# Attention scores from float32 operands in place of three products of split operands

## The chip, the cores and the metric

The kernel runs on one core of one Trainium2 chip. The metric is the device time in microseconds (us) of that core for one execution, the median of several runs. Engines go by the profile's names: PE (TensorE; PEld is its weight loads), DVE (VectorE), ACT (ScalarE), POOL (GpSimd) and SP (SyncE, which here issues DMAs).

## The reference, cut to what matters

```python
def _attn_ref(q, k, v):                    # (4, 12, 448, 64) each
    S = q.shape[2]
    scale = 1.0 / np.sqrt(q.shape[-1])
    scores = scale * np.matmul(q, k.transpose(0, 1, 3, 2)) - np.log(S)
    attn = 1.0 / (1.0 + np.exp(-scores))
    return np.matmul(attn, v).astype(np.float32)

def reference(**kwargs):
...
    attn_out = _attn_ref(**attn_kwargs)
    B, H, S, D = attn_out.shape
    x = np.ascontiguousarray(attn_out.transpose(0, 2, 1, 3)).reshape(B, S, H * D)
    x = _moe_ref(x=x, **moe_kwargs)
    return _moe2_ref(x=x, **moe2_kwargs)
```

Attention is a sigmoid of scaled scores (no softmax) over 448 positions and 48 heads with a head dimension of 64. The two layers behind it take its output: `_moe_ref` is a gated layer whose first product has 768 x 1024 weights (`w_in`), `_moe2_ref` a layer with cosines and sines of a product, a mix over positions and a last product.

## The kernel before

Heads go in pairs, n = 0 to 23, six pairs to a batch element. Head 0 of a pair lies on partitions 0 to 63 and head 1 on 64 to 127 (`halves`), so the two matmuls of a pair, each over 64 rows, use the two row halves of the array. A pair's keys and queries come in one tile `r` of 128 x 2 x 448 float32 (`load_kq`, L165 to L170, 448 KB, four buffers).

Most products of the kernel are made of split operands. An operand is rounded to the type float32r (`hi`), the rest is put into a second tile (`lo`), and three products hi*hi, hi*lo and lo*hi are summed in PSUM. `split_pair` (L177 to L182) does it on DVE for keys and queries: a copy into `kqh` (L181) and a subtraction into `kql` (through the helper at L56), for 23 of the 24 pairs. Pair 0 (`F32_SCORES`) isn't split: its scores are one float32 matmul per head, straight from `r`. A float32 matmul stands in the trace as two records of each of its weight load and matmul, a float32r one as one.

`scores(t, g)` (L189 to L200) makes the scores of 128 keys (g = 0, 1, 2) by 448 queries for both heads into a PSUM tile of two banks (`pss`), and ACT turns it into a sigmoid, 128 x 896, tile `af` (L186). The last 64 keys of two pairs go together in `end_scores` (L202 to L208), float32 from `r` for all pairs. `begin_attend` (L217) and `attend` (L224) multiply sigmoids and values in float32 into `psa`; ACT copies the result to float32r (L62) and DVE subtracts for the low part (L56). `uv` (lines L65 to L67 and L243 to L245) is the first product of the layer behind, float32r, three products each.

PSUM is four tiles of two banks (`banks`), which `pss`, `pse` (end scores), `psa` and `psd` (uv) take in turn. PE, ACT, DVE and SP follow the order in which the program is written for this stage (`manual_schedule`). It has twelve rounds, r = 0 to 11, of two pairs each. A round: end scores of the next two pairs; loads of the pairs of round r + 3; a piece of weight work; attention of the current two pairs; six score groups (three for each of the next two pairs); then weight work again with the two splits of the pairs of round r + 2 in between; then the uv groups that `UV_BY` allows (none in rounds 0 to 2, two or three in each later one). The weight work ("pieces") takes float64 weights as 64-bit words (`wraw`) and puts float32 together on DVE (L99, L101, L111) and ACT (L106); for `w_in` it also splits it. From some 200 us on, the rest of the layers follows, ordered by a planner except for what the program ties down.

The pool `at` holds all of this stage's tiles of attention; the pools of the next stage take its place in SBUF once it is closed.

Of the kernel before, what the change touches and what calls it, by code (L numbers as in the profile page):

```python
# [10 lines left out]
F32 = mybir.dt.float32  # L11
F32R = mybir.dt.float32r
# [6 lines left out]
B, H, S, D = 4, 12, 448, 64  # L19
# [3 lines left out]
P = 128  # L23
# [10 lines left out]
PIN = 3.1415925  # L34
EPS = 1e-6

F32_SCORES = (0,)
NAF = 6
CH_FROM = 1
NX = 12  # L40
NKQ = 3
LOADS = ((1, 0), (2, 0), (2, 0)) + 8 * ((2, 2),)
UV_BY = (0, 0, 0, 3, 5, 7, 10, 13, 15, 18, 20)
NW = 4
# [6 lines left out]
def net(ctx: ExitStack, tc: tile.TileContext, kq, vd, vl, w_in, w_sp, bsp, w_out, w_th, w_tok, w_ch, out):  # L51
    nc = tc.nc
    ve, se, te = nc.vector, nc.scalar, nc.tensor

    def sub(o, a, b):
        ve.tensor_tensor(out=o, in0=a, in1=b, op=ALU.subtract)  # L56
# [22 lines left out]
    halves = (slice(0, 64), slice(64, P))  # L79
# [71 lines left out]
    at = es_l.enter_context(tc.tile_pool(name="at", bufs=2, reuse_waits="tile"))  # L151
# [3 lines left out]
    def banks(name):  # L155
        return ps_1.tile([P, 2, 512], F32, tag="s", name=name)


    def load_ends(b):

        r = at.tile([P, NP, D], F32, tag="vends", name="vends")
        nc.sync.dma_start(r, vl[b])
        return r

    def load_kq(n):  # L165
        b, p = divmod(n, NP)
        t = {"n": n, "a": {}, "fs": n in F32_SCORES}
        r = t["r"] = at.tile([P, 2, S], F32, tag="kqr", name="kqr", bufs=4)
        nc.sync.dma_start(r, kq[b, p])
        return t  # L170

    def load_v(t):
        b, p = divmod(t["n"], NP)
        t["v"] = at.tile([P, 6, D], F32, tag="vr", name="vr", bufs=4)
        nc.sync.dma_start(t["v"], vd[b, p])

    def split_pair(t):  # L177
        r = t["r"]
        hi = t["h"] = at.tile([P, 2, S], F32R, tag="kqh", name="kqh", bufs=NKQ)
        lo = t["l"] = at.tile([P, 2, S], F32R, tag="kql", name="kql", bufs=NKQ)  # L180
        ve.tensor_copy(hi, r)  # L181
        sub(lo, r, hi)  # L182

    def sigmoid(tag, ps, bufs):
        af = at.tile([P, 2, S], F32, tag=tag, name="af", bufs=bufs)
        se.activation(af, ps[:, :, :S], AF.Sigmoid, bias=bias, scale=1.0 / math.sqrt(D))  # L186
        return af

    def scores(t, g):  # L189

        ps = banks("pss")
        c = slice(g * P, (g + 1) * P)
        if t["fs"]:
            for j, a in enumerate(halves):
                te.matmul(ps[:, j, :S], t["r"][a, 0, c], t["r"][a, 1, :], start=True, stop=True)
        else:
            for n, (w, x) in enumerate(("hh", "hl", "lh")):
                for j, a in enumerate(halves):
                    te.matmul(ps[:, j, :S], t[w][a, 0, c], t[x][a, 1, :], start=n == 0, stop=n == 2)  # L199
        t["a"][g] = sigmoid("af", ps, NAF)  # L200

    def end_scores(ts):  # L202

        ps = banks("pse")
        for i, t in enumerate(ts):
            for j, a in enumerate(halves):
                te.matmul(ps[halves[i], j, :S], t["r"][a, 0, L0:S], t["r"][a, 1, :], start=True, stop=True)
        return sigmoid("afe", ps, 2)  # L208
# [3 lines left out]
    def begin_attend(ts, ends, ae):  # L212

        ps = [banks("psa")[:, 0, :] for _ in ts]
        for i, t in enumerate(ts):
            for j, a in enumerate(halves):
                te.matmul(ps[i][a, :S], ends[halves[i], t["n"] % NP // 2 * 2 + j, :], ae[halves[i], j, :],  # L217
                          start=True, stop=False)
        return ps

    def attend(t, ps):
        for c in range(3):
            for j, a in enumerate(halves):
                te.matmul(ps[a, :S], t["v"][:, 2 * c + j, :], t["a"][c][:, j, :], start=False, stop=c == 2)  # L224
        xf = ps[:, :S]
        X = x_p.tile([P, 2, S], F32R, tag="X", name="X", bufs=NX)
        acopy(X[:, 0, :], xf)
        sub(X[:, 1, :], xf, X[:, 0, :])
        b, p = divmod(t["n"], NP)
        if b % 2 == 0:  # L230
            xl[b // 2, p] = x_p.tile([P, 2, 2, LT], F32R, tag="XL", name="XL", bufs=NP + 2)
        ve.tensor_copy(xl[b // 2, p][:, :, b % 2, :], X[:, :, L0:S].bitcast(F32))
        xs[b, p] = X
# [76 lines left out]
    def load_pieces(n):  # L310
        for _ in range(n):
            if pieces:
                loaded.append(pieces.pop(0))
                loaded[-1].load()

    def begin_pieces(n):

        nonlocal finished
        for w in joined:
            w.part_low()  # L320
        finished += len(joined)
        joined[:] = apart
        apart[:] = loaded
        loaded.clear()
        for w in joined:
            w.join()
        for w in apart:
            w.low()
        load_pieces(n)

    def end_pieces():

        for w in joined:
            w.part_high()
        for w in apart:
            w.high()

    def uv_now(n):
        nonlocal groups
        for _ in range(n):  # L340
            if todo and finished >= (KC if todo[0][1] < 4 else 2 * KC):
                uv(*todo.pop(0))
                groups += 1

    R = B * NP // 2
    groups = 0
    with tc.manual_schedule(engines={mybir.EngineType.PE, mybir.EngineType.Activation, mybir.EngineType.DVE, mybir.EngineType.SP}):
        rounds = {0: [load_kq(i) for i in range(2)]}
        load_pieces(2)
        ends = load_ends(0)  # L350
        rounds[1] = [load_kq(2 + i) for i in range(2)]
        for t in rounds[0] + rounds[1]:
            load_v(t)
        split_pair(rounds[0][1])
        for g in range(3):
            scores(rounds[0][0], g)
        ae = end_scores(rounds[0])
        rounds[2] = [load_kq(4 + i) for i in range(2)]
        for t in rounds[1]:
            split_pair(t)  # L360
        for g in range(3):
            scores(rounds[0][1], g)
        for r in range(R):
            b, q = divmod(r, NP // 2)
            cur, nxt, aft = (rounds.get(r + i) for i in range(3))
            if nxt:
                ends_n = load_ends(b + 1) if q == NP // 2 - 1 else ends
                ae_n = end_scores(nxt)
            if r + 3 < R:
                rounds[r + 3] = [load_kq(2 * (r + 3) + i) for i in range(2)]  # L370
            begin_pieces(1)
            end_pieces()
            ps = begin_attend(cur, ends, ae)
            for i, t in enumerate(cur):
                attend(t, ps[i])
            if aft:
                for t in aft:
                    load_v(t)
            if q == NP // 2 - 1:
                todo += [(b, g) for g in range(8) if g != 3 or b % 2]  # L380
            if not nxt:
                break
            ends, ae = ends_n, ae_n
            for t in nxt:
                for g in range(3):
                    scores(t, g)
            begin_pieces(LOADS[r][0])
            if aft:
                split_pair(aft[0])
            end_pieces()  # L390
            uv_now(min(1, UV_BY[r] - groups))
            if LOADS[r][1]:
                begin_pieces(LOADS[r][1])
            if aft:
                split_pair(aft[1])
            uv_now(min(1, UV_BY[r] - groups))
            if LOADS[r][1]:
                end_pieces()
            uv_now(UV_BY[r] - groups)
        while pieces or loaded or apart or joined:  # L400
            begin_pieces(2)
            end_pieces()
# [83 lines left out]
    for i in range(2):  # L486
        t = pa.tile([P, DH], F32R, name=f"vb{i}", bufs=1)
# [452 lines left out]
```

## Time and profile before

| what | value |
|---|---|
| three runs | 625.8, 627.7, 628.8 us; median 627.7 us |
| profiled execution, its time | 626.07 us |
| profiled execution, its span | 624.3 us |
| PE busy | 612.6 us (98% of the span) |
| DVE busy | 415.8 us (67%) |
| ACT busy | 346.9 us (56%) |
| granted clock of PE | 1.00 |

The profile is of one execution. Busy times overlap. Ends of matmuls are modelled and reach over the start of the next, so an engine that shows as busy can still have been waiting: the starts of instructions tell more than busy shares.

### The profile page before, as it was taken

How to read it: one execution, taken by the hardware profiler on the slowest of the kernel's cores; microseconds unless marked ns; L12 is line 12 of the kernel's file. 1: busy time of each engine (PE TensorE's matmuls, PEld its weight loads, DVE VectorE, ACT ScalarE, POOL GpSimd, SP SyncE). 2: the span in 40 equal slices, each digit the busy share in tenths (PEclk: the TensorE clock that was granted, in tenths of full speed). 3: DMA queues.
4: the chain of work that ended last, by engine and by line, in shares of the span. 5: the costliest groups of instructions: out<-in, count | busy, mean ns of one | idle time of the engine just before them, and what ended most of it. 6: DMA issues, size and time to landing. Idle time of an engine off the chain costs nothing.

```text
span 624.3 us, 9178 instructions
## 1 busy us (share of the span) xinstructions
PE 612.6 (98%) x3296; PEld 507.1 (81%) x3296; DVE 415.8 (67%) x798; ACT 346.9 (56%) x588; POOL 23.8 (4%) x42
## 2 busy tenths in 40 slices
PE   6999999999999999999999999999999999899997
PEld 2455667757776688999999999999999999789996
DVE  3899576627663559794231386797776797688875
ACT  5799466564555425274336486666567566362540
POOL 0000000000000100100000000101101101000000
PEclk9999999999999999999999999999999999999999
DMA  8787588857864685865767612464183123354603
GB/s 308 239 266 233 187 237 277 271 170 250 291 212 144 203 287 180 245 207 181 220 198 230 161 39 65 89 215 114 56 247 92 50 102 126 113 191 134 224 29 134
DMA packets 82675, 112.63 MB, mean 180 GB/s; under 512 B 27842, under 2 KB 69188, under 8 KB 82628
## 3 DMA queue, kind: packets, MB, share of 16 engines
q1 hardware_dynamic: 74820, 99.18, 50.6%
q10 hardware_dynamic: 7808, 12.85, 5.9%
q8 instruction: 26, 0.43, 0.3%
q14 instruction: 21, 0.17, 0.1%
HBM read 68.06 MB, written 32.93 MB: 162 GB/s over the span
## 4 chain that ended last, share of the span: by engine, by line
PE 79%; DVE 11%; DMA 4%; ACT 3%; issue 2%; SPq 0%; POOL 0%; ACTq 0%; POOLq 0%; DVEq 0%
PE psa L224 7%; PE pss L199 6%; PE psd L65 3%; PE psd L243 3%; PE ppo L66 3%; PE ppo L67 3%; PE ppo L65 3%; PE psd L66 3%; PE psd L67 3%; PE psd L245 3%; PE psd L244 3%; PE pt L638 3%; PE pt L639 3%; PE pt L637 3%; PE py L678 3%; PE py L679 3%
## 5 line engine op out<-in xcount | busy, mean ns | idle before, releaser
L186 ACT ACTIVATE af<-pss,bias 128x896 f32<-128x896 f32 x72 | 66.1, 1020 | 2.8 <-PE pss L199 2.8
L637 PE MATMUL pt<-thh,XT 128*128 128x384 f32 x168 | 56.9, 338 | 0.3 <-DVE r L644 0.3
L638 PE MATMUL pt<-thl,XT 128*128 128x384 f32 x168 | 56.9, 338 | 0.0
L224 PE MATMUL psa<-af,vr 128*64 128x448 f32 x288 | 56.8, 543 | 0.0
L639 PE MATMUL pt<-thh,XT 128*128 128x384 f32 x168 | 56.8, 338 | 0.0
L224 PEld LDWEIGHTS psa<-af,vr 128*64 128x64 f32 x288 | 19.6, 137 | 36.3 <-issue 35.2
L62 ACT ACTIVATE ev<-psd 128x448 f32<-128x448 f32 (+1 forms) x30 | 17.0, 568 | 52.5 <-PE psd L67 26.0
L111 DVE SCALAR_TENSOR_TENSOR wq<-wraw,wq 128x384 int32<-128x384 int32 (+2 forms) x51 | 28.7, 594 | 23.7 <-ACT wraw L106 23.6
L65 PE MATMUL psd<-X,wih 128*128 128x448 f32 x96 | 35.6, 371 | 0.0
L106 ACT ACTIVATE wraw<-wraw 128x384 f32<-128x384 f32 (+2 forms) x51 | 29.6, 604 | 10.7 <-DVE wq L99 7.4
L66 PE MATMUL ppo<-g,wbh 128*128 128x448 f32 x96 | 35.2, 366 | 0.0
L67 PE MATMUL ppo<-g,wbl 128*128 128x448 f32 x96 | 35.1, 366 | 0.0
L65 PE MATMUL ppo<-g,wbh 128*128 128x448 f32 x96 | 35.1, 366 | 0.0
L67 PE MATMUL psd<-X,wil 128*128 128x448 f32 x96 | 35.1, 365 | 0.0
L66 PE MATMUL psd<-X,wih 128*128 128x448 f32 x96 | 35.1, 365 | 0.0
L56 DVE TENSOR_TENSOR X<-psa,X 128x448 fp32r<-128x448 f32 x24 | 15.0, 624 | 27.8 <-ACT X L62 27.8
L648 ACT ACTIVATE m<-r 128x384 f32<-128x384 f32 x28 | 14.6, 520 | 32.5 <-DVE r L646 32.5
L637 PEld LDWEIGHTS pt<-thh,XT 128*128 128x128 f32 x168 | 31.5, 188 | 1.1 <-DVE r L644 0.7
L638 PEld LDWEIGHTS pt<-thl,XT 128*128 128x128 f32 x168 | 31.6, 188 | 0.4
L101 DVE SCALAR_TENSOR_TENSOR wq<-wraw,wq 128x384 int32<-128x384 int32 (+2 forms) x51 | 30.6, 600 | 1.8
L639 PEld LDWEIGHTS pt<-thh,XT 128*128 128x128 f32 x168 | 31.5, 188 | 0.0
L62 ACT ACTIVATE xr<-xp 128x768 uint16<-128x768 uint16 x28 | 28.4, 1066 | 0.5 <-ACT x L62 0.5
(287 smaller groups left out, 1583.9 us busy)
## 6 DMA issues: line engine op xcount, KB each, us to landing
kqr<-in_kq SPq DMA_DIRECT2D x24, 448.0 KB, 4.6
wraw<-in_w_in SPq DMA_DIRECT2D x12, 512.0 KB, 5.3
x_d<-x ACTq DMA_DIRECT2D x24, 224.0 KB, 3.3
xb<-x_d SPq DMA_DIRECT2D x4, 1344.0 KB, 7.7
xp<-xa SPq DMA_DIRECT2D x56, 96.0 KB, 2.5
y_d<-y SPq DMA_DIRECT2D x24, 224.0 KB, 2.1
out_t<-o SPq DMA_DIRECT2D x24, 224.0 KB, 2.0
vr<-in_vd SPq DMA_DIRECT2D x24, 192.0 KB, 4.5
```

Source lines behind the costliest of these rows:

```text
L62: se.activation(o, a, f)
L65: te.matmul(ps, wh, xh, start=first, stop=False)
L66: te.matmul(ps, wh, xl, start=False, stop=False)
L67: te.matmul(ps, wl, xh, start=False, stop=last)
L101: ve.scalar_tensor_tensor(out=self.q, in0=self.hi, scalar=-(2 ** 31), in1=self.q, op0=ALU.bitwise_and, op1=ALU.bitwise_or)
L106: se.activation(self.lo.bitcast(F32), self.hi.bitcast(F32), AF.Copy, scale=2.0 ** -112)
L186: se.activation(af, ps[:, :, :S], AF.Sigmoid, bias=bias, scale=1.0 / math.sqrt(D))
L199: te.matmul(ps[:, j, :S], t[w][a, 0, c], t[x][a, 1, :], start=n == 0, stop=n == 2)
L224: te.matmul(ps[a, :S], t["v"][:, 2 * c + j, :], t["a"][c][:, j, :], start=False, stop=c == 2)
L637: te.matmul(o, t[:, k, 0, :], thh[:, k, hs], start=k == 0, stop=False)
L638: te.matmul(o, t[:, k, 0, :], thl[:, k, hs], start=False, stop=False)
L639: te.matmul(o, t[:, k, 1, :], thh[:, k, hs], start=False, stop=k == KC - 1)
```

## The change

`scores` makes one float32 product per head for every pair, as it did for pair 0, from `r` as it was loaded. `split_pair`, its tiles `kqh` and `kql` (three buffers each) and its four calls go, and `r` gets eight buffers in place of four.

```diff
-F32_SCORES = (0,)
 NAF = 6
...
-NKQ = 3
...
     def load_kq(n):
         b, p = divmod(n, NP)
-        t = {"n": n, "a": {}, "fs": n in F32_SCORES}
-        r = t["r"] = at.tile([P, 2, S], F32, tag="kqr", name="kqr", bufs=4)
+        t = {"n": n, "a": {}}
+        r = t["r"] = at.tile([P, 2, S], F32, tag="kqr", name="kqr", bufs=8)
         nc.sync.dma_start(r, kq[b, p])
         return t
...
-    def split_pair(t):
-        r = t["r"]
-        hi = t["h"] = at.tile([P, 2, S], F32R, tag="kqh", name="kqh", bufs=NKQ)
-        lo = t["l"] = at.tile([P, 2, S], F32R, tag="kql", name="kql", bufs=NKQ)
-        ve.tensor_copy(hi, r)
-        sub(lo, r, hi)
...
         c = slice(g * P, (g + 1) * P)
-        if t["fs"]:
-            for j, a in enumerate(halves):
-                te.matmul(ps[:, j, :S], t["r"][a, 0, c], t["r"][a, 1, :], start=True, stop=True)
-        else:
-            for n, (w, x) in enumerate(("hh", "hl", "lh")):
-                for j, a in enumerate(halves):
-                    te.matmul(ps[:, j, :S], t[w][a, 0, c], t[x][a, 1, :], start=n == 0, stop=n == 2)
+        for j, a in enumerate(halves):
+            te.matmul(ps[:, j, :S], t["r"][a, 0, c], t["r"][a, 1, :], start=True, stop=True)
         t["a"][g] = sigmoid("af", ps, NAF)
...
-        split_pair(rounds[0][1])
...
-        for t in rounds[1]:
-            split_pair(t)
...
-            if aft:
-                split_pair(aft[0])
...
-            if aft:
-                split_pair(aft[1])
```

## Rows read from the trace of the kernel before

**Rows 1.** Page, part 1: busy us (share of the span) xinstructions.

```profile
PE 612.6 (98%) x3296; PEld 507.1 (81%) x3296; DVE 415.8 (67%) x798; ACT 346.9 (56%) x588; POOL 23.8 (4%) x42
```

**Rows 2.** Stretches: busy us of PE, PEld, DVE, ACT, POOL; granted clock, DMA share, GB/s.

```profile
4.00:20.00 16.00, 14.41 (x80) 6.09 (x82) 7.98 (x12) 10.56 (x13) 0.00 (x0) 1.00 0.96 339
20.00:54.00 34.00, 34.00 (x234) 16.97 (x236) 31.28 (x53) 30.96 (x43) 0.00 (x0) 1.00 0.76 242
54.00:200.00 146.00, 145.72 (x874) 99.42 (x872) 89.55 (x172) 84.72 (x124) 0.00 (x0) 1.00 0.71 228
```

**Rows 3.** PE's waits, 0 to 215 us: total, times, longest.

```profile
PE pss L195 <- DMA kqr<-in_kq: 3.9, 1, 3.9
PE pse L207 <- DMA kqr<-in_kq: 1.5, 1, 1.5
```

**Rows 4.** PE's waits from 200 us to the end: the longest of four.

```profile
PE pa__5430 L832 <- DVE y L59: 1.3, 1, 1.3
```

**Rows 5.** PE by time, round 4: start, duration, instruction.

```profile
70.38 0.98 PE L207 MATMUL pse<-kqr 64*64 64x448 f32 x8
71.18 0.93 PE L217 MATMUL psa<-af,vends 64*64 64x448 f32 x8
72.04 4.73 PE L224 MATMUL psa<-af,vr 128*64 128x448 f32 x24
76.70 0.47 PE L199 MATMUL pss<-kqh 64*128 64x448 f32 x2
77.42 0.37 PE L199 MATMUL pss<-kqh 64*128 64x448 f32 x2
78.03 0.37 PE L199 MATMUL pss<-kqh 64*128 64x448 f32 x2
...
79.89 0.37 PE L199 MATMUL pss<-kqh 64*128 64x448 f32 x2
80.61 0.47 PE L65 MATMUL psd<-X,wih 128*128 128x448 f32 x1
```

**Rows 6.** Float32 instructions of single lines: ns min/median/max, first and last start.

```profile
L195 PEld LDWEIGHTS pss<-kqr x12: 218/329/335, 3.9 to 7.1; 64*128 64x128 f32 x12
L195 PE MATMUL pss<-kqr x12: 536/946/1110, 3.9 to 7.5; 64*128 64x448 f32 x12
L207 PE MATMUL pse<-kqr x96: 536/546/587, 8.0 to 192.0; 64*64 64x448 f32 x96
```

**Rows 7.** PE by time, round 1.

```profile
31.03 0.47 PE L199 MATMUL pss<-kqh 64*128 64x448 f32 x2
...
34.87 0.98 PE L207 MATMUL pse<-kqr 64*64 64x448 f32 x8
35.76 1.87 PE L217 MATMUL psa<-af,vends 64*64 64x448 f32 x8
37.56 4.73 PE L224 MATMUL psa<-af,vr 128*64 128x448 f32 x24
```

**Rows 8.** ACT by time, the sigmoids of round 1.

```profile
32.01 5.50 ACT L186 ACTIVATE af<-pss,bias 128x896 f32<-128x896 f32 x6 [0.31 <-PE pss L199]
```

**Rows 9.** PE by time, round 3.

```profile
53.41 0.48 PE L199 MATMUL pss<-kqh 64*128 64x448 f32 x2
...
55.12 0.47 PE L199 MATMUL pss<-kqh 64*128 64x448 f32 x2 [0.20 <-DVE X L56]
...
57.92 0.50 PE L243 MATMUL psd<-wih,X 128*128 128x512 f32 x1
```

**Rows 10.** DVE's groups of the split: busy us, mean ns, idle before.

```profile
L56 DVE TENSOR_TENSOR kql<-kqr,kqh 128x896 fp32r<-128x896 f32 x23 | 25.1, 1092 | 0.8
L181 DVE CAST kqh<-kqr 128x896 fp32r<-128x896 f32 x23 | 14.3, 621 | 10.6 <-DMA kqr<-in_kq 10.6
```

**Rows 11.** SP by time: DMA issues at the start.

```profile
4.25 4.66 SPq L175 DMA_DIRECT2D vr<-in_vd  x4
10.79 0.81 SPq L169 DMA_DIRECT2D kqr<-in_kq  x2
```

## The prediction

> **What bounds the kernel now.** I began with the page's busy shares: PE is busy for 98% of the span, DVE for 67%, ACT for 56% [rows 1]. That is an average, so I cut the time into stretches [rows 2]. The change touches only the attention stage, to about 202 us. Before 20 us the DMA engines are full (a share of 0.96, 339 GB/s) and PE has gaps. From 20 to 54 us (rounds 0 to 2, no uv work) DVE and ACT are busy for 31 of 34 us, beside a PE that shows no gap. From 54 to 200 us PE is the only full engine: DVE has work for 90 of 146 us and ACT for 85.
>
> Then PE's own waits. Up to 215 us two matter, both for the first loads [rows 3]; after 200 us the longest of four is 1.3 us [rows 4]. So PE's order sets the end, and what a matmul is made longer by reaches the end unless PE was secretly waiting where it is put. Modelled ends hide such waits, so I read starts, round by round.
>
> Round 4 stands for rounds 4 to 10, seven of them [rows 5]. Six score groups run from 76.70 to 80.61 us, 3.91 us: 0.61 to 0.63 us a group, with 0.1 us more at the first and at the last, where the array's layout changes. Uv work follows at once, and nothing there waits for ACT or DVE beyond that 0.1 us.
>
> Round 1 stands for rounds 0 to 2 and differs [rows 7, 8]. From the first score to the first L224 takes 6.53 us against 5.57 us in round 4 (3.91, then 0.80 and 0.86 for L207 and L217). ACT explains it: six sigmoids take 5.50 us from 32.01 us, some 0.9 us apart, the four PSUM tiles fill, and the second half of L217 waits for the fifth sigmoid. There the score block has about 0.9 us of cover.
>
> Round 3 lies between: its block takes 4.51 us (53.41 to 57.92 us) because group three waits for a DVE subtraction [rows 9].
>
> **What the change removes.** On DVE 23 casts and 23 subtractions, 14.3 + 25.1 = 39.4 us [rows 10], about 3.4 us a round. PE is full over the same time and waits for DVE only in round 3, so I cost this at nothing but there. What hides it is PE's own work; without that cover it would be worth the most in rounds 0 to 2. Even there little is to be had: PE's own work for such a round, if it waited for nothing, would with the new block (below) be 4.72 + 0.80 + 0.86 + 4.66 = 11.04 us, against a period of 11.19 us now (from 31.03 us to the end of L224's block, 37.56 + 4.66 us [rows 7, 5]).
>
> On PE 414 float32r matmuls go (23 pairs, three groups, two heads, three products).
>
> **What it adds.** 138 float32 matmuls in their place, 276 records, two of each pair of heads side by side. How long is a group of these? The exact form occurs only in the first 8 us, for pair 0 [rows 6]: 12 records start from 3.93 to 7.5 us and the next line follows at about 8.0 us, six steps of two records in 4.0 us. Their durations are 946 ns in the median and 536 ns at the least; the later float32 matmuls of L207, on the same number of columns, take 536 to 587 ns. Though the granted clock shows 1.00 there, the start so ran at about half of the later rate, as at 1.2 GHz of the two levels. The two heads do overlap: 12 x 842 ns of records would be 10.1 us one after the other.
>
> For the later rate I take the nearest float32 rows of round 4 [rows 5]. L224 has 24 records, two side by side, so 12 steps from 72.04 to 76.70 us, 4.66 us with the layout change at either end: 0.388 us a step. L207 has 8 records, four side by side, two steps in 0.80 us; L217 two in 0.86 us. A score block is 12 steps: 4.66 us by L224, 4.80 by L207, 5.16 by L217. The low bound is L224 less the two layout changes of 0.1 us, 4.46 us. L224 is the nearest, with the same number of steps and a layout change at both ends; I add 0.06 us, as the middle groups now vary from 0.61 to 0.63 us, which I put down to the step into a new PSUM tile. So 4.72 us for 3.91 us: **+0.81 us a block**, between +0.55 and +1.25. Weight loads (218 ns at the later rate [rows 6]) fit in a step of 0.388 us, so I add nothing for them.
>
> **The sum.**
> - Rounds 4 to 10: 7 x 0.81 = +5.7 us (3.9 to 8.8).
> - Round 3: 4.72 for 4.51 us, as the DVE subtraction that it waits for comes earlier, with 3.4 us less ahead of it in DVE's queue: +0.2 us (-0.1 to +0.65).
> - Rounds 0 to 2: the first sigmoid starts some 0.1 us later (a first group of about 0.8 us for 0.72), and the chain of sigmoids covers the rest: 3 x 0.1 = +0.3 us. If the cover fails, 3 x 0.81 = +2.4; at best, 0.
> - Pair 1, before round 0: three groups, about +0.4 us, covered by the 1.5 us for which PE then waits for `kqr` [rows 3]: 0, or +0.4.
> - Eight buffers: the loads of pairs 4 to 7 need not wait for a buffer. Pairs 4 and 5 are issued at 10.79 us though SP was done with `vr` at 8.91 [rows 11]. They go out earlier, behind the same loads as now, so I expect nothing: PE is not waiting for a load after the first 14 us. If they take bandwidth from `kqr` of pairs 2 and 3 or from `vr`, which are under way, one such load at 339 GB/s is 448 KB / 339 = 1.3 us later: 0 to +1.3. Later SP isn't held up by a load of keys, so the weights behind it come sooner; no PE wait hangs on them: 0.
> - Scores wait for a DMA in place of DVE: by then the load is two rounds old, so 0. ACT's work is the same.
> - `at` shrinks by two tiles of 3.5 KB a partition, so the next stage's tiles lie over others. Its first loads over the old place follow the last attention in the program's order, and both move alike: 0. The planner may order the later stages a little otherwise: 1 us either way.
>
> Sum: 5.7 + 0.2 + 0.3 = **+6.2 us**. After 202 us PE goes on without a gap [rows 4], so all of it arrives at the end. Against the profiled execution that is 626.1 + 6.2 = 632.3 us; this execution was 1.6 us under the median of 627.7 us, from which the sum is 633.9. I take **633.0 us**, between them.
>
> **The rivals.** About 0.5% (3.1 us) is what a measurement of this kernel can tell from no change.
>
> *All covered (no change).* If ACT's chain held PE in the later rounds as in rounds 0 to 2, every block would cost 0.1 us: 11 x 0.1 = +1.1 us, 628. For it: sigmoids 0.9 us apart are slower than groups of 0.78 us. Against it: in round 4 uv starts 0.1 us behind the last score and needs one PSUM tile where round 1 needs three; ACT catches up during the two or three uv groups.
>
> *Float32 is cheaper than three products (faster).* It decides at 0.61 us a group: if a group cost one step of 0.388 us, a block would be about 2.5 us, 1.4 us less, and seven rounds give 9.8 us; with round 3's 2.0 us, the block of rounds 0 to 2 being held by ACT, 626.1 - 11.8, about 614 us. For it: a third of the products are left. Against it: each record has its own step, and L224 shows 12 steps for 12 float32 products of 448 columns in pairs. The Trainium skill has both readings: "Perfetto Trace Analysis", section "Engine Utilization", halves the array's output rate for FP32_LOW_HIGH, which taken for the whole product is this rival at an estimate of 614 us, while "FP8 and Floating Point Precision", section "TensorE Precision Notes", counts four passes for true FP32. The trace bears out the four: two records of about 0.388 us a pair against 0.204 us for one float32r step (0.61 us a group, three steps).
>
> *Dearer still (slower).* Steps as in L217 (0.43 us), cover failing in rounds 0 to 2 and a start disturbed by early loads: 8.8 + 0.65 + 2.4 + 1.3 = +13 us, 639. Against it: L217 ends in a layout change after only two steps, which twelve steps spread.
>
> **How the numbers follow.** Forecast (+3.3 to +10 us) 0.67; dearer still 0.13; all covered 0.14; faster 0.06. So slower by over 0.5%: 0.80; within: 0.14; faster: 0.06. The range runs from a sum at the low bounds with half of the covered case, 628.5, to 638.5, short of the dear case at its full price.
>
> **What would show it.** After the change: no L181, DVE about 376 us busy; score blocks in rounds 4 to 10 of 4.7 us with steps of 0.375 to 0.39 us; rounds 0 to 2 with a period near 11.3 us; no wait for DVE in round 3; whatever PE does after 202 us some 6 us later. The prediction is wrong if a group takes under 0.65 us, if uv in rounds 4 to 10 turns out to start behind a sigmoid, or if PE finds new waits for `kqr` in the first 20 us.

## The result and the profile after

The changed kernel takes 632.8 us in the median of four runs (632.5 to 634.1), the kernel before 627.4: a ratio of 1.0091, with a 95% interval of 1.0062 to 1.0120. It is slower. The prediction was 633.0 us, in a range of 628.5 to 638.5. A second pair (`changed_again` below), beside 29 runs of the kernel before, gave a ratio of 1.0082 (1.0059 to 1.0105).

The profiled execution took 632.99 us, its span 631.0. Here are its busy shares (part 1 of the page) and its stretches, against [rows 1, 2]:

```profile
PE 619.6 (98%) x3158; PEld 495.5 (79%) x3158; DVE 377.9 (60%) x752; ACT 346.6 (55%) x588; POOL 24.0 (4%) x42
```

```profile
4.00:20.00 16.00, 14.84 (x72) 5.57 (x72) 3.10 (x6) 10.35 (x12) 0.00 (x0) 1.00 0.96 349
20.00:54.00 34.00, 34.00 (x194) 13.69 (x192) 21.77 (x41) 30.77 (x43) 0.00 (x0) 1.00 0.73 250
54.00:200.00 146.00, 146.00 (x758) 89.80 (x758) 64.17 (x139) 82.60 (x121) 0.00 (x0) 1.00 0.69 225
```

DVE lost 38 us, some 30% of its work to 200 us, and the kernel got longer. PE, full before, is full after, with 138 records fewer and 7 us more. Round 4 on PE, in order of time, against [rows 5]:

```profile
71.39 0.98 PE L193 MATMUL pse<-kqr 64*64 64x448 f32 x8
72.19 0.93 PE L203 MATMUL psa<-af,vends 64*64 64x448 f32 x8
73.05 4.73 PE L210 MATMUL psa<-af,vr 128*64 128x448 f32 x24
77.71 4.78 PE L185 MATMUL pss<-kqr 64*128 64x448 f32 x24
82.42 0.47 PE L63 MATMUL psd<-X,wih 128*128 128x448 f32 x1
```

The score block runs from 77.71 to 82.42 us: 4.71 us for 3.91. Its 24 records last as long as the 24 of L210 above them within 0.05 us, and uv starts right behind, as before. Round 1 on PE, and ACT's sigmoids in it, against [rows 7, 8]:

```profile
31.49 4.78 PE L185 MATMUL pss<-kqr 64*128 64x448 f32 x24
36.20 0.98 PE L193 MATMUL pse<-kqr 64*64 64x448 f32 x8
37.00 1.24 PE L203 MATMUL psa<-af,vends 64*64 64x448 f32 x8
38.17 0.60 PE L210 MATMUL psa<-af,vr 128*64 128x448 f32 x2
```

```profile
32.62 5.50 ACT L177 ACTIVATE af<-pss,bias 128x896 f32<-128x896 f32 x6 [0.47 <-PE pss L185]
```

Here the block is as much longer (4.71 us for 3.84), but L203 now takes 1.17 us for 1.80: it waited for a sigmoid before, and most of the block's 0.87 us has gone into that wait. From the first score to the first L210 it is 6.68 us for 6.53. Six sigmoids still take 5.50 us; the first starts 1.13 us behind the first score for 0.98, and that 0.15 us is what the round gets longer by.

In round 3 the block runs from 54.17 to 58.88 us, 4.71 for 4.51, and the wait for DVE of [rows 9] is gone. PE's waits, to 215 us and after 200 us, against [rows 3, 4]:

```profile
PE pss L185 <- DMA kqr<-in_kq: 4.0, 1, 4.0
PE pse L193 <- ACT af L177: 1.1, 1, 1.1
```

```profile
PE pa__5062 L811 <- DVE y L57: 1.4, 1, 1.4
```

The wait of 1.5 us for keys in pair 1 is now one of 1.1 us that ends with a sigmoid (in the second profile of the changed kernel, 0.9 us for keys again). No other wait is new. SP's issues at the start, against [rows 11]:

```profile
4.27 4.76 SPq L173 DMA_DIRECT2D vr<-in_vd  x4
10.91 3.23 SPq L167 DMA_DIRECT2D kqr<-in_kq  x4
14.34 0.33 SPq L88 DMA_DIRECT2D wraw<-in_w_in  x1
```

The loads of pairs 4 and 5 are not issued sooner, 10.91 us for 10.79, though they have free buffers now. In both kernels SP's wait ahead of them (1.8 us before, 1.9 after) ends when a load of weights (`wraw`) lands.

### The profile page after: what moved, and what is told of

The parts are those of the page before. It is cut to its first block, busy times and chain, and to the rows that moved or that the text cites. A ratio compares the mean times of both kernels' runs of the same rounds, so it can differ in the third digit from the quotient of the medians.

```text
span 631.0 us, 8829 instructions
## 1 busy us (share of the span) xinstructions
PE 619.6 (98%) x3158; PEld 495.5 (79%) x3158; DVE 377.9 (60%) x752; ACT 346.6 (55%) x588; POOL 24.0 (4%) x42
## 4 chain that ended last, share of the span: by engine, by line
PE 83%; DVE 7%; DMA 5%; ACT 3%; issue 1%; SPq 0%; POOL 0%; ACTq 0%; POOLq 0%; DVEq 0%
PE psa L210 9%; PE pss L185 8%; PE psd L63 3%; PE psd L229 3%; PE ppo L63 3%; PE ppo L64 3%; PE ppo L65 3%; PE psd L64 3%; PE psd L65 3%; PE psd L230 3%; PE psd L231 3%; PE pt L617 3%; PE pt L618 3%; PE pt L616 3%; PE py L657 3%; PE py L658 3%
## 5 line engine op out<-in xcount | busy, mean ns | idle before, releaser
L185 PE MATMUL pss<-kqr 64*128 64x448 f32 x288 | 59.6, 560 | 4.0 <-DMA kqr<-in_kq 4.0
L210 PE MATMUL psa<-af,vr 128*64 128x448 f32 x288 | 56.8, 543 | 0.0
L185 PEld LDWEIGHTS pss<-kqr 64*128 64x128 f32 x288 | 27.4, 192 | 35.2 <-issue 28.5
L210 PEld LDWEIGHTS psa<-af,vr 128*64 128x64 f32 x288 | 19.6, 137 | 36.3 <-issue 36.1
L616 PEld LDWEIGHTS pt<-thh,XT 128*128 128x128 f32 x168 | 31.5, 188 | 1.2 <-DVE r L623 0.8
```

What stands on the lines that cost most here:

```text
L616: te.matmul(o, t[:, k, 0, :], thh[:, k, hs], start=k == 0, stop=False)
```

## Where the time went

Starts on PE add up the whole difference. The first score of round 0 starts at 20.15 us for 19.84, the last attention (its first matmul, L203, L217 before) at 215.50 for 209.26. The recorded expectations call this last point the end of attention.

| piece | after less before, us |
|---|---|
| start, to the first score of round 0 | +0.31 |
| rounds 0 to 2 (34.02 for 33.57) | +0.45 |
| block of round 3 | +0.20 |
| blocks of rounds 4, 5, 6, 8, 9, 10 (4.71 for 3.85 to 3.91) | +4.88 |
| block of round 7 (4.88 for 4.68) | +0.20 |
| uv of all rounds | +0.20 |
| attention stage with the start | +6.24 |
| later stages | +0.5 |
| span (631.0 for 624.3) | +6.7 |

For the experiments two lengths are taken from each profile: the **attention stage**, from the first score of round 0 to the start of the last attention, and the **later part**, from the uv block behind that attention to the end of the span. The start is in neither. The ratio is to the kernel before on the same chip, with its 95% interval.

| run | attention stage, us | later part, us | ratio |
|---|---|---|---|
| before | 189.42 | 409.5 | |
| before_again | 189.51 | 413.5 | 1.0011 (0.9992 to 1.0031) |
| after | 195.35 | 410.0 | 1.0091 (1.0062 to 1.0120) |
| changed_again | 195.32 | 411.2 | 1.0082 (1.0059 to 1.0105) |
| splits_kept | 195.56 | 412.0 | 1.0130 (1.0108 to 1.0153) |
| four_buffers | 219.51 | 411.6 | 1.0492 (1.0461 to 1.0523) |
| fourth_product | 198.49 | 411.1 | 1.0159 (1.0134 to 1.0184) |
| float32_early | 189.68 | 414.6 | 1.0072 (1.0049 to 1.0096) |
| float32_early_again | 189.78 | 411.1 | 1.0024 (1.0004 to 1.0044) |
| float32_late | 194.88 | 410.2 | 1.0064 (1.0041 to 1.0087) |
| one_product | 194.43 | 411.4 | 1.0036 (1.0004 to 1.0068) |
| late_copy | 189.25 | 409.3 | 0.9977 (0.9948 to 1.0007) |
| after_late_copy | 195.15 | 409.7 | 1.0057 (1.0024 to 1.0090) |
| early_and_late_copy | 188.80 | 415.8 | 1.0016 (0.9999 to 1.0033) |

The attention stage repeats within 0.1 us for each of the three programs that were profiled twice. The later part does not: 409.5 and 413.5 us for the very same kernel. What an edit of the attention stage does is therefore read from that stage, and the ratio only says whether it can be seen in the whole.

## The experiments

**Is DVE's relief worth anything?** The changed kernel, with the splits left in and nothing reading them.

```diff
+    def split_pair(t):
+        r = t["r"]
+        hi = at.tile([P, 2, S], F32R, tag="kqh", name="kqh", bufs=1)
+        lo = at.tile([P, 2, S], F32R, tag="kql", name="kql", bufs=1)
+        ve.tensor_copy(hi, r)
+        sub(lo, r, hi)
...
+        split_pair(rounds[0][1])
...
+        for t in rounds[1]:
+            split_pair(t)
...
+            if aft:
+                split_pair(aft[0])
...
+            if aft:
+                split_pair(aft[1])
```

> Float32 scores as in the change, but DVE still splits all 23 pairs into high and low tiles that nothing reads. Theory A (the change's cost is the longer score blocks where PE is the bound; the 39 us taken from DVE bring nothing but the wait in round 3): between 0 and 0.8 us above the changed kernel, 633.0 to 633.8 us; score blocks of rounds 4 to 10 stay at 4.71 us, only round 3's block is over 4.71. Theory B (freeing DVE won time, and the blocks cost more than the net shows): at least 2 us above the changed kernel, 635 us or more.

The two groups of DVE work are back (by line):

```profile
L54 DVE TENSOR_TENSOR kql<-kqr,kqh 128x896 fp32r<-128x896 f32 x23 | 25.1, 1092 | 0.8
...
L179 DVE CAST kqh<-kqr 128x896 fp32r<-128x896 f32 x23 | 14.3, 622 | 10.4 <-DMA kqr<-in_kq 10.3
```

The block of round 4 runs from 77.22 to 81.93 us, 4.71 us as in the changed kernel. 39.4 us of DVE work cost the stage 0.21 us (195.56 for 195.35), all of it in round 3, whose block took 4.93 us for 4.71. The ratio is 0.4% above the changed kernel's: its interval overlaps that of the first pair and just misses that of the second (1.0105 against 1.0108), on a chip whose runs of the kernel before were faster (625.5 us). In time it is 1.0 us above the changed kernel, between theory A's 0.8 and theory B's 2. The profile puts 2.0 us more into the later part, where PE, DVE and ACT follow the order of the kernel before; whether the splits have a share in that is not shown. For the attention stage theory A stands and theory B falls.

**Do passes count, or the type?** The kernel before with a fourth product.

```diff
-            for n, (w, x) in enumerate(("hh", "hl", "lh")):
+            for n, (w, x) in enumerate(("hh", "hl", "lh", "ll")):
                 for j, a in enumerate(halves):
-                    te.matmul(ps[:, j, :S], t[w][a, 0, c], t[x][a, 1, :], start=n == 0, stop=n == 2)
+                    te.matmul(ps[:, j, :S], t[w][a, 0, c], t[x][a, 1, :], start=n == 0, stop=n == 3)
```

> The kernel before with a fourth product, low by low, for the 23 split pairs: the number of passes that theory A ascribes to one float32 product, without float32. Theory A (passes count, not the type): a group is 4 x 0.204 = 0.82 us, a block 5.1 us for 3.9; six full blocks +7.1 us, rounds 7 and 3 +0.5 each, rounds 0 to 2 some +0.3 each: +9 us, 636.4 us. If float32 itself were what is dear, a further step in each group would cost less than the change: under 632 us.

Round 4 on PE, the first record of groups one, two and three, and uv:

```profile
78.04 0.47 PE L199 MATMUL pss<-kqh 64*128 64x448 f32 x2
...
78.97 0.37 PE L199 MATMUL pss<-kqh 64*128 64x448 f32 x2
...
79.79 0.37 PE L199 MATMUL pss<-kqh 64*128 64x448 f32 x2
...
83.19 0.47 PE L65 MATMUL psd<-X,wih 128*128 128x448 f32 x1
```

A group takes 0.82 us and a block 5.15; the stage grew by 9.07 us, as forecast. One float32 product of a pair of heads, 0.75 us a group without the layout changes (two steps of 0.376 us in the trace after), lies between three float32r products (0.61) and four (0.82).

**Where does it cost, where is it covered?** Float32 for pairs 0 to 7 alone, and for pair 0 and 8 to 23 alone. Both have six buffers for `r`, and split only what is not float32.

```diff
-F32_SCORES = (0,)
+F32_SCORES = tuple(range(8))
...
-        r = t["r"] = at.tile([P, 2, S], F32, tag="kqr", name="kqr", bufs=4)
+        r = t["r"] = at.tile([P, 2, S], F32, tag="kqr", name="kqr", bufs=6)
...
-            if aft:
+            if aft and not aft[0]["fs"]:
                 split_pair(aft[0])
```

```diff
-F32_SCORES = (0,)
+F32_SCORES = (0,) + tuple(range(8, 24))
```

> The kernel before with float32 scores for pairs 0 to 7 alone (pair 1 and rounds 0 to 2, where ACT's chain of sigmoids covers PE), six buffers for keys and queries; the other pairs split. Theory A: rounds 0 to 2 have periods of 11.34 us for 11.19 (+0.45 us), the start +0.3 at most, and round 3's wait for DVE goes (-0.6): 627.4 us within 0.5 us, no change. If the cover doesn't hold, 20 groups at 0.17 us make +3.4 us: 630.8 us.

> The counterpart of the run with early pairs: the kernel before with float32 scores for pair 0 and pairs 8 to 23 (rounds 3 to 10), six buffers; pairs 1 to 7 split. Theory A: blocks of 4.71 us in rounds 4 to 10, so six times +0.80 and +0.2 in round 7, round 3 +0.2 to +0.8: +5.5 us when attention ends, near the whole change. If the change's cost lay in the first rounds or in the loads of the start, under +2 us. The later stages have moved by up to 5 us between the runs so far with nothing changed in them, so the attention stage is read from its own starts.

Round 1 of the early run and round 4 of the late run, on PE:

```profile
30.23 4.78 PE L195 MATMUL pss<-kqr 64*128 64x448 f32 x24
...
36.91 4.73 PE L224 MATMUL psa<-af,vr 128*64 128x448 f32 x24
```

```profile
76.83 4.78 PE L195 MATMUL pss<-kqr 64*128 64x448 f32 x24
81.55 0.47 PE L65 MATMUL psd<-X,wih 128*128 128x448 f32 x1
```

Early: from the first score to the first L224 it is 6.68 us, as in the changed kernel. The stage grew by 0.26 us: a period of 11.34 us in round 0, as theory A had it, and 0.13 us back in round 3, where theory A had 0.6. Late: +5.46 us. The two together make 5.72 of the change's 5.93 us. The cost is in the rounds with uv work, and the cover in the others holds.

The early run's time missed its expectation all the same: 0.7% up where no change was expected, 630.5 us where 630.8 stood for a cover that doesn't hold. The stage shows that the cover held. The profile ends the last attention 0.7 us sooner than before, and takes 5.1 us more in the later part. So it was run once more, and the kernel before too.

> The run with float32 for pairs 0 to 7 alone once more. In the first run the attention stage ended 0.7 us sooner than before, yet the time was 0.7% up, since the later stages took 414.6 us for 409.5. If that is a property of this program (its other layout in SBUF and other times of loads), again 413 us or more and a ratio of 1.006 or more; if it was the day of that chip, 409 to 412 us and a ratio within 0.5% of 1.

> The kernel before once more, for a second profile: how much its later stages differ between executions with nothing changed. First profile: 409.5 us from the last block of uv to the end. If they vary by themselves, between 409 and 412 us; if they are steady and the differences of other runs come from their edits, 409.5 within 0.2 us. Ratio 1.000.

> The changed kernel once more, beside its own runs of the kernel before, for a second profile and a narrower interval. Theory A: attention ends (second half of the last L203) near 215.2 us, 6 us later than before; the later stages, whose instructions are the same in the same order, within 1.5 us of the kernel before; +6 to +7 us in all, a ratio of 1.010. If the later stages had been changed by the edit, their part would come out 0.5 us longer again.

The start of the last attention and of the uv block behind it on PE, in the second profile of the kernel before:

```profile
209.23 0.98 PE L217 MATMUL psa<-af,vends 64*64 64x448 f32 x8
...
214.80 0.47 PE L65 MATMUL psd<-X,wih 128*128 128x448 f32 x1
```

It reaches the last attention at 209.23 us, as in its first profile (209.26), and its span is 4.0 us longer: 413.5 us from 214.80 us on, for 409.5. In the second run of the early variant the later part fell from 414.6 to 411.1 us and the ratio to 1.0024. So the later part varies by some 4 us without an edit, and the 5.1 us can't be read as the edit's. The largest of PE's waits after 216 us, in the second profile of the kernel before, stands at another line than in [rows 4]:

```profile
PE pt L637 <- DVE r L644: 2.1, 2, 1.9
```

Behind such a wait the granted clock can fall. These are the stretches behind the wait of 1.9 us at L637, in the second profile of the kernel before, and behind one of 2.3 us at L834, in the first of the early variant (in the second, behind one of 1.8 us, it stays at 1.00):

```profile
512.00:516.00 4.00, 4.00 (x16) 3.93 (x16) 4.00 (x10) 3.48 (x7) 0.00 (x0) 0.63 0.24 86
552.00:556.00 4.00, 4.00 (x13) 3.55 (x13) 2.56 (x5) 0.00 (x0) 0.00 (x0) 0.57 0.78 251
```

In the first of them 18 matmuls of L637 to L639 take 4.81 us for 3.27 in the first profile, so 1.5 of the 4.0 us come with the lower clock and the rest with waits. The early variants meet this more often than the kernel before. All three of their profiles have a wait of 1.8 to 2.3 us at L834 (L839 with the late copy), where the first profile of the kernel before has 0.4 us. A mean granted clock under 0.998 stands in 12 of the 16 runs of the early variant, in 6 of 12 of the early variant with the late copy (below), and in 15 of the 70 runs of the kernel before in these experiments. In the second early run those eight took 630.2 us in the mean and the four others 627.9, as in the kernel before on that chip (a median of 628.0). Whether early float32 causes this, and what makes those chains late in one execution and not in another, was not tested.

**Do the eight buffers matter?** The changed kernel with four.

```diff
-        r = t["r"] = at.tile([P, 2, S], F32, tag="kqr", name="kqr", bufs=8)
+        r = t["r"] = at.tile([P, 2, S], F32, tag="kqr", name="kqr", bufs=4)
```

> The changed kernel with four buffers for keys and queries in place of eight. Theory A: no PE wait hangs on these loads after the start, so 632.8 us within 1 us, though the loads of round r + 3 now wait for the scores of round r. Theory C (the early loads that eight buffers allow disturb the start): attention begins again at 15.2 us in place of 15.5, and the time is 0.3 us lower. A third way, that the weights queued on SP behind the waiting loads come late and hold ACT and then PE in rounds 0 to 3: 2 to 10 us above the changed kernel.

The stage grew by 24.2 us over the changed kernel. The order of the program puts the loads for round r + 3 ahead of the scores of round r. With four buffers those scores must have read the tile before the load can start. SP's issues show it held up from 10.39 us:

```profile
10.39 14.23 SPq L167 DMA_DIRECT2D kqr<-in_kq  x4
24.68 1.50 SPq L88 DMA_DIRECT2D wraw<-in_w_in  x1
```

The weights behind these loads are issued at 24.68 us in place of 14.34. Waits of 20 to 80 us:

```profile
DVE wq L97 <- DMA wraw<-in_w_in: 32.0, 6, 8.3
...
PE pss L185 <- DVE X L54: 9.7, 3, 4.0
```

DVE waits for the weights, its subtraction that frees a PSUM tile stands behind them, and PE waits for that tile: the third way of the expectation, at more than twice its upper price. In rounds 1 to 3 the score blocks take 9.9 to 10.8 us, and the granted clock falls with PE's waits:

```profile
30.00:34.00 4.00, 2.86 (x14) 0.71 (x10) 3.41 (x7) 2.06 (x3) 0.00 (x0) 1.00 0.42 169
34.00:38.00 4.00, 2.15 (x8) 1.01 (x10) 3.31 (x7) 3.88 (x7) 0.00 (x0) 0.78 0.00 0
```

**Why did round 7 cost so little?** Its block took 4.68 us before the change. In DVE's order of time there (kernel before) a copy waits 6.6 us for uv, with the subtraction behind it that frees a PSUM tile. The block doesn't wait for that subtraction itself, which starts 1.2 us after the block's end (139.54 us). Its last three groups start 0.9 us apart, near the pace of the sigmoids, as if one tile too few were free. First PE's fourth and fifth group, then DVE:

```profile
136.85 0.47 PE L199 MATMUL pss<-kqh 64*128 64x448 f32 x2
...
137.75 0.47 PE L199 MATMUL pss<-kqh 64*128 64x448 f32 x2
```

```profile
140.55 0.23 DVE L232 CAST XL<-X 128x128 fp32r<-128x128 f32 x1 [6.62 <-PE psd L245]
140.69 0.62 DVE L56 TENSOR_TENSOR X<-psa,X 128x448 fp32r<-128x448 f32 x1
```

The copy was moved behind both subtractions, in the kernel before and in the changed one.

```diff
-        ve.tensor_copy(xl[b // 2, p][:, :, b % 2, :], X[:, :, L0:S].bitcast(F32))
         xs[b, p] = X
+
+    def ends_x(t):
+        b, p = divmod(t["n"], NP)
+        ve.tensor_copy(xl[b // 2, p][:, :, b % 2, :], xs[b, p][:, :, L0:S].bitcast(F32))
...
                 attend(t, ps[i])
+            for t in cur:
+                ends_x(t)
```

> The kernel before with the copy of the last positions (L232) of both pairs moved behind both subtractions (L56) of a round. In round 7 this copy waits 6.6 us for uv, and the second subtraction, which frees a PSUM tile, stands behind it. Theory A: this is why round 7's block takes 4.68 us before the change and hid most of its cost; the block falls to 3.91 us and attention ends 0.8 us sooner. If the tile isn't what the block waits for, 4.68 us as before.

> The changed kernel with the same move of the copy. Theory A: round 7's block of 4.88 us falls to 4.71 us only, as float32 groups now set it, 0.2 us. If the tile still decides, a larger fall. The rest of the attention stage is as in the changed kernel: it ends 6.0 us later than in the kernel before.

DVE and PE in round 7 of the kernel before with the copy moved, then PE in the changed one:

```profile
135.91 0.62 DVE L56 TENSOR_TENSOR X<-psa,X 128x448 fp32r<-128x448 f32 x1 [1.63 <-ACT X L62]
```

```profile
135.22 0.47 PE L199 MATMUL pss<-kqh 64*128 64x448 f32 x2
...
139.13 0.50 PE L246 MATMUL psd<-wih,XL 128*128 128x512 f32 x1
```

```profile
137.94 4.78 PE L185 MATMUL pss<-kqr 64*128 64x448 f32 x24
142.65 0.50 PE L232 MATMUL psd<-wih,XL 128*128 128x512 f32 x1
```

The subtraction comes at 135.91 us, the block takes 3.91 us (135.22 to 139.13) and 4.71 us with float32: it was the tile. The stage gained only 0.17 us in the kernel before, not 0.8, as round 3's block took 5.11 us for 4.51 in this run. PE waits 1.00 us there for DVE's subtraction (0.20 us in [rows 9]); DVE had waited 0.65 us for weights ahead of it, at 46.00 us, which it didn't in the profile of before. Whether the moved copy has a part in that was not tested. In the changed kernel it gained 0.20 us, as expected.

**Does less work on PE reach the end?** One product in place of three.

```diff
-            for n, (w, x) in enumerate(("hh", "hl", "lh")):
+            for n, (w, x) in enumerate(("hh",)):
                 for j, a in enumerate(halves):
-                    te.matmul(ps[:, j, :S], t[w][a, 0, c], t[x][a, 1, :], start=n == 0, stop=n == 2)
+                    te.matmul(ps[:, j, :S], t[w][a, 0, c], t[x][a, 1, :], start=n == 0, stop=n == 0)
```

> The kernel before with the first of the three products alone (high by high) for the 23 split pairs; it leaves out the two others, so the scores have the precision of the rounded operands. It asks how far shorter PE blocks reach the end. Theory A: PE's part of a block falls from 3.9 to 6 x 0.204 + 0.2 = 1.4 us, but uv then waits for the third sigmoid, some 3.3 us behind the block's start, so a block gains only 0.6 us: 7 x 0.6 = 4.2, and rounds 0 to 3 some 1.5 more: about -5 us against the kernel before. If PE alone decided, -2.5 us in each of 11 blocks: -27 us.

Both forecasts fell: the stage got 5.0 us longer, with two thirds of the score work of 23 pairs gone. The blocks did what theory A said (3.41 us in round 4, set by the third sigmoid): rounds 0 to 2 and the blocks behind them gained 4.1 us. The loss lies behind the blocks, where uv took 9.1 us more. Round 3 on PE in order of time, then the stretches of 51 to 68 us and, last, the block of round 4:

```profile
53.63 0.47 PE L199 MATMUL pss<-kqh 64*128 64x448 f32 x2 [1.77 <-DVE X L56]
54.30 0.69 PE L199 MATMUL pss<-kqh 64*128 64x448 f32 x4 [0.20 <-ACT af L186]
...
56.10 0.80 PE L243 MATMUL psd<-wih,X 128*128 128x512 f32 x1 [0.15 <-ACT af L186]
56.69 0.63 PE L244 MATMUL psd<-wil,X 128*128 128x512 f32 x1
57.12 0.63 PE L245 MATMUL psd<-wih,X 128*128 128x512 f32 x1
```

```profile
51.00:56.00 5.00, 2.76 (x14) 1.08 (x12) 4.38 (x10) 4.75 (x8) 0.00 (x0) 0.88 0.89 330
56.00:60.00 4.00, 3.90 (x9) 3.13 (x10) 3.80 (x7) 4.00 (x7) 0.00 (x0) 0.50 0.66 214
60.00:64.00 4.00, 4.00 (x15) 3.19 (x15) 3.90 (x8) 0.96 (x2) 0.00 (x0) 0.80 0.38 98
64.00:68.00 4.00, 4.00 (x19) 3.30 (x18) 0.78 (x1) 0.60 (x1) 0.00 (x0) 1.00 0.17 66
...
77.00:81.00 4.00, 2.65 (x17) 1.16 (x14) 2.77 (x7) 3.41 (x5) 0.00 (x0) 1.00 0.52 182
```

PE waited between its groups (busy 2.76 of 5 us), the granted clock fell to 0.50, the lower of its two levels (1.2 of 2.4 GHz), and uv behind it ran at 0.43 us a matmul, for 0.23 in the kernel before, until some 61.4 us: 15.05 us of uv for 12.45. The same follows in rounds 6, 7, 9 and 10 (14.10, 13.20, 14.09 and 9.06 us for 12.48, 11.62, 12.48 and 7.49). The kernel before shows 1.00 in all these stretches. But the blocks of rounds 4, 5 and 8 wait as well (PE busy 2.65 of 4 us in round 4), and there the clock stays at 1.00 and uv takes 7.49, 7.50 and 7.63 us for 7.49. So a thinned block was followed by the lower clock in five rounds of eight; what tells them apart was not tested. The Trainium skill ("TensorE: Matmul & The Clock Gate", section "What's actually happening") has an activity monitor set the clock by how busy the engine has been, with the throttled state as the default. This run agrees in the five rounds, the lower clock behind the thinned block and 1.00 once uv had run on; the three others don't show it.

**What the runs point to.** Float32 in rounds 0 to 2 (with round 3's lighter DVE queue) and the late copy, the rest split: the diffs of the early run and of the late copy in one kernel.

> What the runs point to as the quickest attention stage: float32 for pairs 0 to 7 where ACT covers it (no splits there, and no wait for DVE in round 3) and the copy L232 moved behind both subtractions (round 7's block at 3.91 us); the rest split as before. Theory A: attention ends 1.4 us sooner than in the kernel before, at 207.8 us; the whole 0.2% faster if the later stages stay as they are, which is below what the median can tell.

The last attention starts at 207.76 us, 1.5 us sooner than in the kernel before, where 1.4 were expected; but 0.9 us of that is an earlier start (18.96 us for 19.84), which varies without an edit (18.89 and 19.75 us in the two profiles of the early variant). The stage is the shortest of all, 188.80 us. The time is not: 1.0016, from 0.9999 to 1.0033, with 415.8 us in the later part of its profile, whose clock shows 0.57 at 552 to 556 us as above. It beats the changed kernel and not the one before.

## Why the prediction was right

Point by point, by its own steps:

- *What bounds the kernel*: PE's order. Right: work taken from DVE brought 0.2 us to the stage, and work put on PE came out at its end wherever PE was the full engine.
- *The price of a group*, taken from L224 at 4.72 us a block: 4.71 us. L224's row gave it though it has other weights and another layout of the array. The 0.06 us that was added for new PSUM tiles was right by luck: the steps between tiles are 0.376 us like the others, and what the block has over L210's is its first step (77.71 to 78.19, 0.48 us for 0.43). The Trainium skill counts four passes for true FP32 ("FP8 and Floating Point Precision", section "TensorE Precision Notes"); the group of 0.75 us is 3.7 float32r steps of 0.204 us, near that.
- *Seven blocks of +0.81*: +5.08 us, not 5.7. The step that was off is "Round 4 stands for rounds 4 to 10": round 7 took 4.68 us already, for a reason that the trace of before showed in DVE's order of time.
- *Rounds 0 to 2*, +0.3: +0.45, and covered by ACT's chain as said; the run with early pairs alone shows the same. *Round 3*, +0.2: +0.20.
- *Pair 1 and the start*, 0: +0.31 us in one profile and, in the second pair, the first score of round 0 at 19.68 us for 19.72. The +0.31 arises by 8.27 us (7.96 before), in pair 0, which the change leaves as it was. Pair 1 cost nothing, as said: from its first score to the next end scores it is 3.60 us for 3.61.
- *Eight buffers, nothing*: right that they brought nothing. The reason given, that four loads would go out earlier, was wrong for pairs 4 and 5: they go out as late with free buffers, since SP waits for a load of weights to land ahead of them, not for a buffer. What the prediction did not say is that the change needs the added buffers: with four it takes 4.9% more than the kernel before.
- *The later stages*, 0 to 1 us either way: they moved by 0.5 us in one profile and -2.3 us in the second pair, and by 4 us in the unchanged kernel. That term was too narrow, and it fits the forecast by luck as much as by reasoning: the attention stage made +5.9 us where +6.2 stood.

Of the rivals, "all covered" is refuted by the late run (+5.46 us), "float32 is cheaper" by the step in the trace after, and "dearer still" by blocks of 4.71 us and cover that held.

## What to carry to other kernels

Price a new matmul form from the nearest form in the same trace, by the distance of starts over a whole block with its layout changes, and multiply it only by the blocks in which PE is the engine that waits for nothing; go through these one by one, as one of seven was not like the others. Taking work from an engine that is not the bound is worth what the bound engine waits for it, here 0.2 us of 39. And taking work from the bound engine can cost time where the next limit then makes it wait and its clock falls.

## What was not expected of the hardware

- With one score product in place of three, and the gaps that waits for ACT and DVE then left, the granted clock fell to its lower level behind the blocks of five rounds of eight (some 3 to 6 us each, an estimate from the mean clocks of the stretches). That cost more than the work saved: a stage of 194.4 us for 189.4.
- The part of the kernel after the attention stage, the same instructions in the same order, took 409.5 us in one execution and 413.5 us in another, 1.5 us of it by a granted clock of 0.63 behind a wait of 1.9 us, while the attention stage repeated within 0.1 us.
